# PSUM banks read from a table of their own in a table-ordered conformer block

## The chip, the cores and the metric

The kernel runs on one core of a Trainium2 chip. The metric is the device time in microseconds of one execution of the whole program. A core has five instruction streams: TensorE (PE, with weight loads shown apart as PEld), VectorE (DVE), ScalarE (ACT), GpSimd (POOL) and SyncE (SP, which here only issues DMAs). Each stream is executed strictly in the order in which the program lists it; an instruction that needs another engine's result waits on a semaphore, and everything listed behind it on its own engine waits with it.

## What is computed

A conformer block over `x` of shape (2, 4000, 144), bfloat16, with four heads of width 36:

```python
h = layernorm(x);  x = x + 0.5 * (silu(h @ w_ff1a) @ w_ff1b)          # 144 -> 576 -> 144
qkv = layernorm(x) @ w_qkv                                            # 4 heads of 36
p = softmax(q @ k.T * 36 ** -0.5);  x = x + (p @ v) @ w_o             # 4000 x 4000 per head and sequence
a, b = split(layernorm(x) @ w_pw1);  h = a * sigmoid(b)
c = depthwise convolution of h over 5 neighbours with dw
x = x + silu(c) @ w_pw2
h = layernorm(x);  x = x + 0.5 * (silu(h @ w_ff2a) @ w_ff2b)
out = layernorm(x)
```

Almost all of the work is the attention: 4 heads x 2 sequences x 4000 x 4000 scores, each of which is multiplied out, exponentiated, and multiplied with V.

## The kernel before

**Tiles.** The 8000 tokens are 16 chunks of 500 (8 per sequence), and a chunk is four blocks of 125 tokens. The keys of a sequence are 63 tiles: 62 of 64 keys and one of 32. One step of the attention takes one chunk of queries and one tile of keys for all four heads. Four matmuls of 64 x 64 weights and 500 columns (`PS<-QT,KT`) write the scores into a pair of neighbouring PSUM banks, two heads in each. Then one engine exponentiates the pair into a buffer `PT`: ScalarE in one ACTIVATE of 128 x 1000 (`emit_exp`), or VectorE in five cheaper operations that work one bank at a time (`dve_tile`). Then four matmuls (`PS<-PT,VA`) add the product with V to two accumulators, in banks 6 and 7, which are held through all key tiles of a chunk and then emptied (`epilogue`). There are 1008 such steps, 841 on ScalarE and 167 on VectorE.

Everything else is background work that is laid in between: layer norms (statistics on VectorE, `ST` and `RS`, the power on GpSimd), transposes through TensorE (`PS<-IDENT,XN`), the first feed-forward and the projections to Q, K and V (`ff1`, `pre2`), and behind the attention of a chunk its output projection, gated unit, convolution and second feed-forward (`post1`, `post2`). A feed-forward tile is two matmuls (`PS<-XT,WA`), a tanh on ScalarE (`TH<-PS`) and a product on VectorE (`HT<-TH,PS`); the way back to 144 columns is 20 short matmuls (`PS<-WB,HT`) and two additions on VectorE (`X<-PS,X`).

**PSUM.** A core has eight banks. Two are the accumulators. The other six, 0 to 5, serve the scores and all background tiles: a step on ScalarE takes two neighbouring ones (`take_pair`), everything else takes one (`take`). In the tail, behind the last attention step, bank 6 joins them.

**The order.** The program is not written down by hand: the kernel's Python plays the block through first. `Sched` holds the background jobs as generators, `pick` chooses at each step what goes next from modelled start times, `Rec.op` records each instruction with a modelled cost, and `Banks` hands out the bank that has been free the longest. `Rec.op` also finds what an instruction depends on. Its table `hist` keeps, for each key (a buffer, or `("ps", bank)`), the last writers and readers. An instruction that writes a bank depends on all who read the tile that was in it before.

What comes out is cut into blocks, one for each step of the planner and engine. Then `Rec.reorder` moves whole blocks on their engine by the table `ORDER`: one letter for each block, whose place in `ALPHABET` less 45 is the number of places by which it moves (P stays, Q goes one later, O one earlier). The dependencies stay those of the planner's play, so two tiles that the planner gave the same bank keep their turn. `Rec.finish` turns dependencies into semaphore waits and leaves out those that another wait already covers; `Rec.replay` (line 284) issues every instruction, which is why the profile gives all of them this one line.

Of the kernel before, what the change touches and what calls it, by code (L numbers as in the profile page):

```python
# [37 lines left out]
        "RPRPRRGRMOQRSQSQYIPY[GPZR[IR[GRZRY[SABBQVRUU?AEFTKPRRLMPPQRROUQJNOOPPSOPQMPPPPPPPPPQRRMNPPQSPMQNQOSO"
        "ORNOPPPPPQQNROOPQOPSPNRNOQOPPPPPPPPPPPPPPPPPPPPPPPPPPTOPNOQOTOPNVNOVNPMMOOPQOTOPSMPMQOPPQOPQOPPPPPPP"
        "PPPROOTOTPMMRNTPMORRMWPLUPVLOVQUHQHVQITQIMMPPPPPRORPMPQOPPPRRNNQOPRTQNLOPQQNPRPNQQNRPRPUPJOOOPQRNOQQ"  # L40
        "NQQRMQNPPUPNSVMMUPKMNQQMQOPSPNRNOQOTOSPMMQOQQNPQQNPSOOOPPPPPPPPPQQNPQOPQQNROOPPPPPPQOQOPPSOOOPPPPPPP"
        "PPPQOPROOSSNNRMTNOORNTNOORNTRMNSMPNSOPNTOPNQQQLQRNOQRNTNUNOSLNNQQRRLQMQQQMQOQOPPPUOPPPLQXNOOPPPPKPRS"
        "QMRLRNQSMORNWNPPQLPRTKPRSKRSSJRURISTISPSTHTHSPSJRSSHSQJRRSIRSKPSKSNSMNRNVPQQKRRRRIRJRRRLRRRJRRKRMRRM"
        "RM[QMPQXKOOOJXNLQQQKTTTINKRRSJRXKQQQJXOJPQLVOLPQLUMTOORRJQSPIQNQUNPPRLNSSNSMMOSSNNSPLQRMQRMQRRLQRLRR"
        "MQRRRJWRPJPUKTMULMMSOMQRRLSPLQRRLSPLRRMSPLRRRLWQKPPQKUPLPRRLSQRJQRKSPMQRMSPMQQRLSQMQVLPPQUKRLOMPPQOR"
        "SSSMKMPQQNUOOOOOWOOOOPPMUVNNNOMRNOQRNOQSPPLPPPPQQNQOPSOOQQMPPQOPPPPPPPPPPPPPPPPQOPPPPQQNPPPPQQQMQOPP"
        "PPPPROOROQNPPPPPPRPNPPPPPPPPPPPPPPPPPPPQOPPPPPPQOPQOPPPQOPPPPQOPPTOOOOPPSOOOPPQOPPQOPQOPSPNRPRPTQINO"
        "PPPPPPROQUMOOPNSOORPMRPNQOPRPNQQQMPPQQNPSOOQNPQOPQOPQOPSSNNNPQOPSSNNNQQNROOQQQMQQNPQOPQQQMRPNPRRN[MO"
        "PPMYNNNNVNLNOMVNPPPLVNUPULOKLQNQRNQRMUWMNNNNPQTLPRMQTLOPRMQSMORRMQQLPQORRNNPQQQSLOOPQOROOPROOPPQOQQN"
        "QQQMQRNOROOSOOQNQOQQQMQQNQQRMQQMQOQQQMQQQMQSNOQRMRNQQMPQRSOLQRMQQRLQQQLRPQMRPNROOQQNROOROOQOUOTQMMMQ"  # L50
        "RNRPMQQNPQQNROOPQQNPQQNROOPQOROOPPPPQQNPPQTNOPNRPRMOPQQNPPQQNQOQQNQQQQLROOQOQQQMQOQQQMQQQMQOPQQRMQNR"
        "PNQORPNQQNQQQMSQRNRKOPQQNROOPQQSSLRNLQOQQNQQNQQSMOQNRPSMRNNSOOZNOOOOPPMRXNLPNTUPLLLQNPQOQQNROORPNQOQ"
        "QQQQKQQQMPPRPQQQKQQNROQNPPPPPPPPPPPPQOQOPPPPPPPPPPQOPPPPPPPQOPPQOPQOPPPQOQOROOSOOSNOQNQOQQQMPPROOPPP"
        "PPQQNPPSOOOPQOPPPPPPQSNOOPQOPPPQQQMRPNPPXQNNOOPNOPTQNNOXOOOPNOORNQQSLPNQQNPPPPQQQMPQQNPQOPPPPPPQOPPP"
        "QQNRPUPPSJNNPQOPPPPPPPPPPPUOQNNQQQLQQNPPPPPPPPQQSPLOQOPRPNPQOTOPNOQOPPROQSMORNOPQOQOQOPQQNPPPQOQOQOP"
        "QQNPQOQQNQOQOQQNQQQMROOQQNQQQMSPNOQOSOOOQOPPQOPPPQOPPPQQQQQKRSQMMPROOPQRRMNPSSNNNPPPPRRRRSQRRRGGPPPP"
        "PPPPPPPPQQNPPPPPPPPPPPPPPPPPSOOOPPQOPPQOPPQOPPPPTPNOOQOQOPQQNPPQOPPPPPPPPPPPPPPPPPPPPPPPPPPPQQQQLQOP"
        "PPQOROOPQOPPQORPNQOPPQOQOPQQQRLQRMQQMPQOPROOQQNPQQNRPNPPPPSOOOPPQOPPQOPRPNQORPNQQNRPNQOPPQOPPSOOOPPP"
        "PPPPQOPPQOPQQNPSSNNNQQQMQQRMQQMQOQQNROOPPPQQQMPQVNOUNNNRMNPSPPQLQQNRPNSOPSSSNJVPPJUNNTMNRMNZPPPLPNRP"
        "MMPPPSPNOPSOPNSPNOQOPQOQOQOPROOQQNPQTNOOOPQRNQQRLQRMQQMQQRMQNQQSMRNNPRRRRUKQJRMRRLQMRRORLOPQOPQQNPQQ"  # L60
        "QMPPPPPPQOQQRMOPPPPRRNNPQORROMQQRMRNOQQQQLROOQQQMPPPPPPPROOPPQOPQOPPQOPQOPPQOPPQQNPQOSOOOPROOPPPQOQQ"
        "NPPPQQNPPPPPPPPPPQOPPPPPPPPPPPPPPQOPPPQOPQQNPPPQQNUOOOOOQOQOROOQOPPPRPQQLPPPQOPQOPQQNPPQOPPPQOPTOOOO"
        "SOOTNOOZNPXMNOULPLLLQQNRPRMOROOPVOOOOOOROQNPROQSMPRMQNQOPPPPPQOPPPPPQOPPPPPPPPRPNPQQNROOPPPPPPQQNQOP"
        "PPPPPPPPPQOPPSSNNSMROMQQQMPPPPPPPPPPPQOQTNPNQNPQRNQRRLSMPQRRSJRRKSPKQQRLQQMQOPQQNSSNNNPQOPQOPQOPVOWN"
        "QULQSSISQGIQQNVOSUSTKKTJJSSSSSMIRHOPQQNPROOQOQRPMPQSPPLQOSPNOROOPPPSOPNPPROOPROOPPPPPQQN"
    ),
    "act": (
        "PPPPPPPPPPPQRNOPPPPPPPPQOPPPPPPPPPROQNPPPPQOPPPPPPQOPQOPPPPRORNOPPPPPPPPPPPPPPPPPQQNPPPQOQOPPPPPPPPP"
        "PPPPPPPQOPPPPQOPPPPPPPPPPPPPPPPPPPPPPPPPPPPPPPPPPPPPPPPPPPPPPPPPPPPPQOPPPPPPPPQOPQOPPQOPQOPPPPPPPPPP"
        "PPPPPPPPPPPPPPPPPPPPPPPPPPPPPPPPPPPPPPPPPPQOPPPPQOPROOPSOOOPPPPPPPPPPPSSNNSMOOPPPPPPRSNNOPPPPPPPPPPP"  # L70
        "PPPPPPPPPPRRNNQQNPPPPPPPPPPPPPPPPPPPPPPPPPPPPPPPPPPPPPPROOPPPPPPPPPROOROOPPQOQOPPPPPPPPPPPPPPPPPPPPP"
        "PPPPPPPPPPPPPPPPPPPPPPPPPPPPPPPQOPPPROOPPPPPPPPPPPPPPPPPPPPPPQOPPPPPPPPPPPPPPPPPPPPPPQOPPPPPPPPPPPPP"
        "PPPPPPPQOPPPPPPPPPQQNPPQOPPPPPPPPPPQOPPPPPPPPPPPPPQOPPQOQOPPPPQOPPPPPPPQOPPPPPPPQOPPQOPPPPPPPPPPPROO"
        "PPQQNPPPPPQOPPPQOPPQOPPPPPPPPPPPPPPPPPPPPPPPPPPPPPPPPPPPPPPPPPPPPPROOPPPPPPPPPPPPPPPPPPPPPPPQOPPPPPP"
        "PPPPPPPPPPPPPPPPPPPPPQOPPPPPPPPQOPPQOPPPPPQQNPPPPPQOPPPQOPPPPPQOPPPPPPPPPPPPPPPPPPPPPPPPPPPPPPPPPPPP"
        "PPPPPPPPPPPQOPPPPPPPPPPQOPPPPPPPPPPPPPPPPPPPPPPPPPPPPPPPPPPRPNPPPQRNOPPPPPTOOOOPQOPPPPPPPPPPPPPPPPPP"
        "PQOPQOPPPPPPPPPPQOPPPPPPPPPPPPPPPPPPPPPPPPPPPPPPPPPPPPPPPPPPPROOPQOPPPPPQOPPQOPPPPPPPQOPPPQOPPPPPPPP"
        "PPPPPPPPPPPPPPPPPPPPPPQOPPPPPPPPPPPPPROOROOPQOPPPPPPPPPPPPPPPPPPQQNPPQQQMPPQOPPQOQQQQQQJPQO"
    ),
    "dve": (  # L80
        "PPQOPPQOPPPROOcOOOR`MMMNQMMMPMMZOMTPPHUQRLTRPWRBOTEOMNPSOOOQOPQQQSQKQMWRPNLOOOPPPPPTOOOQNPPPVPPQQTQQ"
        "TTFPGRRRNQRGQNPUPRUNKMXNYMOQOKOQJNPPR[NNOYNZMMMMMMQQKRKRNOPQOPPPQOQQNPQOQSNOOPQOPPPPPPPPPPPPPPPQRRRR"
        "KRKQNRPNPTPPPTPTOOSOPQRPQQQQQQQQSPSS5RSQRTJSSESSKRJ^PPJOOOOOOOQNNQOPQOPPPPPROQNQOPPPPPPQOQOQOPPTRSMR"
        "LQKPPPPPQQNQOPPPPPPPPPPPPPQOPPPPPPPPPPQOQOQOPQOSQNNRVNNPN`NNOOOPNZNNNNNNNNOOQOPPPPQQQMPQOROSNRNQMPPP"
        "PPPPPPQQNPPPPPPPPPSPNOROOQOPPPPPPPSOOOPTPPSLPSPKSNORNORPNSPNSNOSNROMPPPPPRPNROOQOROQQMQOPQOQORPNROOR"
        "OQQQLPPPQOPPQOPQOPSOPNQOPQQNPQOPPPPPRPSMPNROORPNPRPNQOQQN[OPNQNNPNOPNPPPROOPPPQOPPPPPPPPPPPPPPPPPPPP"
        "PPPPPPPQOPPPPPPPPPPQOPPPQOPPPPPPPPPPPPQQNPPPPPPQOQRPSPKOPPPPPQOPQOPPPPPPPQOPPPQOQOQOPPPPPPPPPQQNPPQO"
        "PPUOOOTOTLNNRNOSOPSPLRNQNPPPPQRNOPPPPPPPPPPPPPPPPPPPPPRRRMQQKPSOTOMOQNPPPPPPPPPPROQNPQOPPPQOPPPPPPPP"
        "PPYOOOOOOOOORTRMMNPPPPPPPPPPQOQOPPPPPPPPPQOQOPQQRMQQQQQQSHPQMPPQOPQQQMPQQNROUNOOOOPQOPPPPPPPPQOUOPNO"
        "OPTOQRMMPPPPPPPPPPPPPPPPPPPPPPPPPPPPVPQMPPLPQQQMPPPPPPQOPPQOPPPPPPQOPPPPQOPPPPPPPQOQOPQOPSPNRNOQQNQR"  # L90
        "NOPSOPNoOOOOOOOOOOOOOOOOOOOOOPNOOOPNPNQOPPPPPPPPQOPROOROOSPROQKPPPPPPPPPPRPRMQQQQKPPQOPQQNPPPPPPPPPP"
        "PPPQOPPPPPPPPPPPPPQQNPPQOPPP_OOOOROQLPLPNPNPWORNNNPNPPPPPPQOPPPPPPPPSORORLOPPQORPNPQOPQQQMQOPPPPPPPQ"
        "QQMPPPQOPQOQRNQNPQOPPPPPPPQOQOPPQQQRPKPPQQNPQQNPRPQMPPPPPPPPPPQOPPPPPROQNPRPNROOQOPQOQQNPQOPQORPQQLR"
        "RNQMPPSPNOPPTPNPQQLQQNPPPPPPPPPPPPPPQOQOPPPPQOPPPQOPPPPQOQOPPPPPPQOUOPNRNQMPPROOPPPPPPPPPPPPPPPPPPPQ"
        "QRPQQQIPPROOPROQNQOPPPQQNPPQOPPPPPPPPPPPPROQNPRPQMQOPPPPPPPPPPPPPPPPPPQOPQOPPPPQQQMPRORPRPKPPPPPPPPR"
        "OQQQLPPRPNPPPPPPPPPPPPPQOPPPPP^ROSLPLPLOOOOOROOQTTPLMNPQOPQRTOPROISOOOWPQORPNQHQOPTOSOTLMOORPNQOPQOP"
        "PPPPPPPPPQQQM"
    ),
# [12 lines left out]


# [1708 lines left out]
```

## Time and profile before

| | |
|---|---|
| median of three runs | 910.52 us (910.25 to 910.66) |
| the profiled execution | 910.27 us, span 908.5 us |
| granted TensorE clock | 0.998 of full speed |
| instructions in the profile | 27,451 |
| TensorE matmuls and weight loads | 11,946 each |
| ScalarE / VectorE / GpSimd busy | 871.8 / 807.8 / 276.1 us |
| exponential on ScalarE, 128 x 1000 | 825 times, mean 1060 ns from start to end |
| exponential on VectorE, 128 x 500 | 334 halves, mean 671 ns for the first operation |

How to read it: instructions of one engine overlap at their ends, so the mean duration of an instruction is longer than the distance at which they follow each other, and busy time counts overlapped time once. Matmul ends are modelled. A wait in the table of waits is idle time of the waiting engine, put down to the instruction that came last. The chain is followed back from the last instruction of the program, at each step to what released it.

### The profile page before, as it was taken

What the parts mean: (1) busy time and instruction counts of PE and PEld (TensorE: products, weight loads), DVE (VectorE), ACT (ScalarE), POOL (GpSimd) and SP (SyncE); (2) the same over time, 40 slices, a digit from 0 to 9 for tenths busy, and PEclk for the clock granted to TensorE, in tenths of its full rate; (3) what the DMA queues carried; (4) which work ended last, traced back from release to release, by engine and by line L of the source; (5) the groups of instructions that cost most, each with busy time, mean ns of one, the idle gap of its engine ahead of it and who ended that gap; (6) DMA issues with size and microseconds to landing.
All of it is one profiled execution on the core that took longest, in us unless ns stands there. A gap on an engine that the chain in (4) does not pass through costs nothing.

```text
span 908.5 us, 27451 instructions
## 1 busy us (share of the span) xinstructions
PE 883.6 (97%) x11946; PEld 410.0 (45%) x11946; DVE 807.8 (89%) x1756; ACT 871.8 (96%) x1105; POOL 276.1 (30%) x519
## 2 busy tenths in 40 slices
...
## 3 DMA queue, kind: packets, MB, share of 16 engines
...
q10 hardware_dynamic: 1416, 0.62, 0.3%
...
## 4 chain that ended last, share of the span: by engine, by line
ACT 50%; PE 43%; DVE 5%; issue 1%; DMA 0%; POOL 0%; POOLq 0%; DVEq 0%
ACT PT L284 45%; PE PS L284 43%; ACT TH L284 5%; DVE PT L284 2%; DVE ST L284 1%; DVE HT L284 0%; DMA X<-in_x_dram 0%; POOL RS L284 0%; DVE X L284 0%; DVE KT L284 0%; DVE QT L284 0%; DVE VA L284 0%; DVE U L284 0%; DVE XT L284 0%; DVE XN L284 0%
## 5 line engine op out<-in xcount | busy, mean ns | idle before, releaser
L284 ACT ACTIVATE PT<-PS 128x1000 bf16<-128x1000 f32 (+1 forms) x841 | 776.9, 1052 | 6.6 <-PE PS L284 3.7
L284 PE MATMUL PS<-QT,KT 64*64 64x500 bf16 x3968 | 418.7, 385 | 11.8 <-ACT PT L284 7.4
L284 PE MATMUL PS<-PT,VA 64*37 64x500 bf16 x4636 | 401.7, 373 | 1.6 <-DVE QT L284 0.8
L284 DVE TENSOR_SCALAR PT<-PS 128x500 int16<-128x500 f32 x334 | 222.4, 671 | 25.0 <-PE PS L284 22.6
L284 PEld LDWEIGHTS PS<-QT,KT 64*64 64x64 bf16 x3968 | 122.7, 104 | 220.3 <-ACT PT L284 119.8
L284 PEld LDWEIGHTS PS<-PT,VA 64*37 64x37 bf16 x4636 | 134.1, 96 | 93.3 <-DVE PT L284 20.7
L284 POOL TENSOR_SCALAR RS<-ST 125x4 f32<-125x4 f32 x112 | 34.1, 304 | 465.3 <-DVE ST L284 459.5
L284 DVE TENSOR_SCALAR PT<-PT 128x1000 uint16<-128x1000 uint16 x334 | 136.1, 417 | 2.6
L284 POOL TENSOR_SCALAR XN<-X,RS 125x144 bf16<-125x144 bf16 x224 | 130.9, 596 | 6.5 <-DMA out_dram<-XN 0.8
L284 POOL TENSOR_TENSOR RS<-RS,NHALF 125x4 f32<-125x4 f32 (+1 forms) x101 | 95.5, 950 | 92.7 <-DVE RS L284 87.9
L284 DVE TENSOR_TENSOR PT<-PT 128x1000 bf16<-128x1000 bf16 x167 | 112.8, 678 | 1.9
L284 ACT ACTIVATE TH<-PS 128x500 bf16<-128x500 f32 (+3 forms) x198 | 104.4, 547 | 6.0 <-PE PS L284 4.5
L284 DVE SCALAR_TENSOR_TENSOR HT<-TH,PS 128x500 bf16<-128x500 bf16 (+1 forms) x135 | 81.5, 618 | 19.2 <-ACT TH L284 18.5
L284 PE MATMUL PS<-XT,WA 72*128 72x500 bf16 (+2 forms) x280 | 71.9, 359 | 0.4 <-DVE VA L284 0.2
L284 DVE SCALAR_TENSOR_TENSOR X<-PS,X 125x288 bf16<-125x288 f32 x128 | 57.5, 452 | 13.3 <-PE PS L284 11.9
L284 DVE BATCH_NORM_STATS2 ST<-X 125x6 f32<-125x288 bf16 (+1 forms) x160 | 66.3, 448 | 0.9 <-DMA X<-in_x_dram 0.6
L284 PE MATMUL PS<-WB,HT 128*125 128x144 bf16 (+1 forms) x640 | 52.3, 230 | 0.1
L284 PEld LDWEIGHTS PS<-WB,HT 128*125 128x125 bf16 (+1 forms) x640 | 44.2, 136 | 14.0 <-issue 5.4
L284 DVE COPY XT<-PS 72x1000 bf16<-72x1000 bf16 (+2 forms) x65 | 40.1, 618 | 5.6 <-PE PS L284 4.9
L284 PE MATMUL PS<-IDENT,XN 125*72 125x125 bf16 x512 | 42.9, 221 | 1.3 <-DVE XN L284 1.0
L284 PEld LDWEIGHTS PS<-IDENT,XN 125*72 125x72 bf16 x512 | 32.0, 112 | 20.5 <-issue 10.9
L284 PEld LDWEIGHTS PS<-XT,WA 72*128 72x128 bf16 x280 | 19.7, 97 | 31.5 <-DVE HT L284 7.7
...
## 6 DMA issues: line engine op xcount, KB each, us to landing
...
```

Of the source, the lines that this page charges most:

```text
L284: ins = getattr(eng, o.name)(*o.a, **o.k)
```

## The change

The bank of a tile is no longer the one that the planner hands out. The planner still plays with its own numbers, now called slots; `Banks.take` and `take_pair` give out `Place` objects, integers that carry the real bank, the slot and the number of the tile. The real bank is read from a new table: `PLACES` holds one figure for each of the 1778 tiles, in the order in which the planner takes them, and a pair takes that bank and the next. `Rec.plain` maps a key back to its slot, so that `hist`, and with it every modelled time and every choice of the planner, is the same as before.

While it records, `Rec.sort` notes for each dependency whether it is there only since two different tiles share a slot (`shared`) or for a reason of its own (`own`). `Rec.reorder` drops the first kind. Then it goes through TensorE's list in its new order, finds for every tile which tiles were last in its banks, and lets its TensorE instructions depend on all instructions of other engines that touch those tiles. So a bank's turn follows the final order of TensorE, not the planner's.

All five strings of `ORDER` are replaced as well: the string for TensorE has 2885 letters in place of 2888, ScalarE 1095 in place of 1091, the others keep their length. Of TensorE's letters some 1,750 differ from those before; 1,794 blocks move (before: 2,065).

```diff
 ORDER = {
     "pe": (
-        "PPPPPPQOPPPPPPPQOPPPQQQQLPPPPQOPRPNRPNQQNPPPWOfNNNcMQMPMINPNLNNOMOMNNPTPNOOPPPPRPNPPROORRUMMPNRTMNRO"
+        "PPPPPPPPPPPPQQRROKPPPPQQNQOQOPQOPPPPQOPRPNQOeOxRMMzPRKLHMNROMKMEOQLJOOQOIQKNQKMOOKOMOMNOOQNQQLQTNOYN"
...
 }
+PLACES = (
+    "0354231433401042510103542035202535024054032151540442105303210412543053121304124010241122402043124032"
...
+    "2140205240240120420421412041204120412041204021402420154250420524025405240524025405240524052405230423"
...
+    "052405245052402402102243002642340643521630254350615436214506230156245130546130"
+)
 
+class Place(int):
+    pass
 
 class Rec:
     def op(self, eng, name, *a, r=(), w=(), q=None, cost=0.1, kind=None, lat=None, **k):
...
+        o.tile, o.shared, o.own = None, set(), set()
+        for key in tuple(r) + tuple(w):
+            if isinstance(key[1], Place):
+                o.tile = key[1].no
         for key in r:
-            h = self.hist.setdefault(key, ([], []))
+            h = self.history(key)
             o.deps += [(d, True) for d in h[0]]
+            self.sort(o, key, h[0])
             h[1].append(o)
...
+    def place(self, slot, n):
+        no, at = len(self.tiles), int(PLACES[len(self.tiles)])
+        self.tiles.append(tuple(range(at, at + n)))
+        out = []
+        for j in range(n):
+            p = Place(at + j)
+            p.slot, p.no = slot + j, no
+            out.append(p)
+        return tuple(out)
+
+    def plain(self, key):
+        return (key[0], key[1].slot) if isinstance(key[1], Place) else key
+
+    def sort(self, o, key, ds):
+        for d in ds:
+            if d is not o:
+                other = isinstance(key[1], Place) and d.tile is not None and d.tile != o.tile
+                (o.shared if other else o.own).add(id(d))
 
     def reorder(self, table):
...
             lines[e] = [o for blk in at for o in blk]
+        users = {}
+        for o in self.ops:
+            drop = o.shared - o.own
+            o.deps = [(d, raw) for d, raw in o.deps if id(d) not in drop]
+            if o.tile is not None and o.eng != "pe":
+                users.setdefault(o.tile, []).append(o)
+        last, prior = {}, {}
+        for o in lines["pe"]:
+            k = o.tile
+            if k is None:
+                continue
+            if k not in prior:
+                prior[k] = {last[b] for b in self.tiles[k] if b in last}
+                last.update({b: k for b in self.tiles[k]})
+            for p in prior[k]:
+                o.deps += [(d, False) for d in users[p]]
...
 class Banks(Slots):
     def take(self):
         i = self.choose()
         del self.free[i]
-        return i
+        return self.R.place(i, 1)[0]
 
     def take_pair(self):
         i = self.pair()[2]
         del self.free[i], self.free[i + 1]
-        return i, i + 1
+        return self.R.place(i, 2)
```

More of the change, by code (lines that the diff above doesn't have):

```diff
@@ L36 @@
     "pe": (
-        "PPPPPPQOPPPPPPPQOPPPQQQQLPPPPQOPRPNRPNQQNPPPWOfNNNcMQMPMINPNLNNOMOMNNPTPNOOPPPPRPNPPROORRUMMPNRTMNRO"
[L38 to L65, printed above, removed]
+        "PPPPPPPPPPPPQQRROKPPPPQQNQOQOPQOPPPPQOPRPNQOeOxRMMzPRKLHMNROMKMEOQLJOOQOIQKNQKMOOKOMOMNOOQNQQLQTNOYN"
@@ new lines @@
+        "NOSQTQKKTPQRSQWQ^BRW`EPWQ[GQ[EQ]RY]S?BBRWSZU?CCFUGQVTHKKNQSPPXPHQQNLOSNPQMPPPPPPQOPRRRMMPPPTPNPNQOSO"
+        "PQMPPQOPPPPPPQOPQOQSNPRPLQOPPPPPPPPPPPPPPPPPPPPPPPPPPQOPPPPPQOPPQOPQOPPPPPPPPQOPPQOPPPQQNPPQOPPPRPRP"
+        "RROIQOSQSQLLQOSOPNQQNSOOUPTLPVQUJQIWQKSQIMMTPPPLTPPROQSQHRMOQOPROOPPQOROOQQNPROOQQNQOPPTOOOOPPPPPPQQ"
+        "NPPPPQQNPPQOPQQNPQOPPPQOPQOPQOQOPPPPPPPPPPPPPQOPQOPPPPPPPPPPPPPPPPPPPQSNPQRLOPPPPPPPPQOPQQNPPPPPQOPP"
+        "PQQNPPPQTNOOQNPPPPPPPPPPPPPQRPMQOPPQOPPTOOPNQQNPROOSSNNNUPNSNOMQQQRLUNOOOOROOPROOPPPPQOPSPNQNQQQMPPS"
@@ new lines @@
+        "OOQNPPPRPNQOUPNOPNPPROOQQNQQQMPRPNQRNQNPQORPQMQOPQQNQOPPPQOPPPPPPPPPQOPQOPQQNPPPPPPPPPPQOPPPTOOOOSOP"
+        "RPSKOOQTNOORNTPMORRMRRRKRLRRRLRRKRRRKSQKRRLTPLTOMRNQMQQSMSNROLQQSMOOQQNQQNQSNPRRLNROOQQNPQOQQQMSPNQQ"
+        "MQQQRLQQQLQSNROULPNRNNQQQMROOQQQMRPNQQNQQNQQQMQRNQQRLQRMQQRLRPSLPRMSPMQRMSPMQRRLQRLQQMQRRTLPLTNOPRMQ"
+        "QQTKPNQQTLPNQQRLQNQQRRRKTTKNNQMRPNPPPPQOQQNQOPROQNQOPQOQOQOPQQNPPPPPPPPPPPPPPPPPPPPPPPPPPROOPPPPQOPP"
+        "PPPPROOPSOPNPPPPPPROOPPPPPPPPPPPPPPPPPPQOPPPPPPQOPQOPPQQNPPPPPPPPPQOPPPPPPPPPPPPPPPPQOPPSPNRPRPQQIPP"
@@ new lines @@
+        "WOOOOQRMQRKOQOQWNOQNNRNNROQNQOPQQNPPPQOPPPPQOPPPROOPPPPPPPPPPPQOPPPPPPPPPPPPPQOPPPPPQOPPPQQNPPPPPPPP"
+        "PPPROOPPRPNPPPPPPPPPPPPPTOQNNPPPQOPQOTUPMMNOQQSMOQNQTNOORNQSMOQSMSOMQQMRROMQSSSSKMKQQNPRPNROOPPPPQQN"
+        "PQQNPQOPSPNOPPSOOOPPPPROOPPQOPPPPPPPPPPPPPPPPPPPPRSQSLLOPPQOPQOPQQNPPQOQOQOQOPPQOQOPQOPQOPPPPPPPPPPP"
+        "QOPQOPPPPPPPQOPPPQOPPPPPQOPPPQOQOSQNQQLPPPPPPPPRORNOPPPPPPPQOPPPQOQQQQLROOQOQQQMQOQQQMQQQMQOQQQQLPPP"
+        "PPPPPPPPPPPPPPQOPPQOQOPRPNPPPPPQRNVNOQNNQNRPNQQSMOQNRPQMRPNSOOQNQOPPPSOOTNOOOPQOQQQQLPQOQQNROOQQNQOQ"
@@ new lines @@
+        "QQQQKQQQMPPRPQQQKQQNROQNPPPPPPPPPPPQQNQOPPPQQNSPNOPPSPRRLMPQOPPQOPQOPPPQOQOROOSOOSNOQNQOQQQMPPROOPPP"
+        "PPQQNPPSOOOPPPPPPPPPPSOOOPPPROOQQRMQNPQOPPPPQQNPPPPPPPPPPPPQOPPQOPPSOOOPQOTQNNOPQOPPQOQQNPPPPPUPNYNY"
+        "MMNVNUOPSHIIPQOPPPQQNPQOPPUOQNNQQQLPPPPPPPPPPPQQSPLOQOPRPNPQOTOPNOQOPPROQRMOPQOSOPQMROOQQNPPPRPNPQOP"
+        "PPPPPPPPPPPPPPPPPPPPPPPQQNPPQOPPPPQOPPPPPPPPPPPPPPPPTPPPQQQITUSMMMMQOQOQQNRRSSLLNQOPROOPPPPQOROOPPQQ"
+        "QQQKPPQQQQLPPPPPPPPPPPPPPPPPPPPPPPPPPPPPPPPPPQQNSQNTRLNQMPPQOPPQOQOPPPPSSPSQKKQOQQQMQQQMQQQMQRNOQOPQ"
@@ new lines @@
+        "RNOSPNQQQLQQQMQOQQNPQQNPPPQQQQLRVNNOOOOPRSNNQQMQQQMTOOOOPPPPSQNNQOPPQOPRPNPPTRNNNPRPNQOPPQOPPSOOOPPP"
+        "PPPPPQOPQOPQQNPSSNNNPQQNPQRNQQMQOQQNROOPPQQQQLPQSNOQNQRNOSORNNQOPQOQOPQOPPQRPMQTTMNNNSOOQNPPQOQOPPPQ"
+        "OPROOPQOPPPPPPPPPPPPPPPPPPPPSOPNQOPPRPNQOPPQOPQQNQQNRPNPQQNQOQQQMROOQOPRRSMRLRMQQMQOSPPRLOPQOPQQNPPP"
+        "QOPPPPPPPPPPPPPPPPPRRNNPPPPRPNRPRMRNOPPQQNROOPQQNPPPPPPPPRPNQQNROOPQSNOQNPRRNSPLQNPQOPPQOPPQOPPPQOQQ"
+        "NPPPQQNPPPPPPPPPPQOPPPPPPPPPPPPPPQOPQOQOQOQOPPPPPPPPQOPPPPPPQOQOQOPPQOROOQQQQLQQNQRRMQMROOPQQNQRPMQO"
@@ L66 @@
+        "ZQOXLNNWMPXKKOUIOLNNQSNPNQQNROOPVOOOOOOQOROQQMQRPMQOPPQOPPPPPQOPPPPPPQOPPPPQOPQOSOPQMROOPPPPQOPPPPPP"
+        "PPPPPPPPUOQNNRSMNSNROMPPQOPPPPPPPPPPPQOPQOQOQOPPQOQRRMRMOQRRRLTPKRNNQQQMPSOOOPQQNPSOOOPPPQOPPRPNVPUM"
+        "QSLRRRIRRGNPQOZOPX_WKLPKKKKQQQSPGUIOOPNPQOROOPPPQOPSQOMPPPPPPPPPPPPROOPPPROOPQOPPPPQO"
     ),
     "act": (
-        "PPPPPPPPPPPQRNOPPPPPPPPQOPPPPPPPPPROQNPPPPQOPPPPPPQOPQOPPPPRORNOPPPPPPPPPPPPPPPPPQQNPPPQOQOPPPPPPPPP"
-        "PPPPPPPQOPPPPQOPPPPPPPPPPPPPPPPPPPPPPPPPPPPPPPPPPPPPPPPPPPPPPPPPPPPPQOPPPPPPPPQOPQOPPQOPQOPPPPPPPPPP"
@@ L70 @@
[L70 to L78, printed above, removed]
+        "PPPPPPPPPPPPROOPQQNPPPPPPPPPPPPPQRSMNOPPPQOQQNQOQQSMPSMOOPPQOQOPPPPPPPPPPPPPPPPPPQRNOPROOPPPPPPPPPQO"
@@ new lines @@
+        "PPPPPPPPPPPPPPPPPPPPPPPPPPPPPPPPPPPPPPPPPPPPPPPPPPPPPPPPQOQQNQQNPPPPQOPPPPPPPPPPPPPPPPPPQOPPPPPPPPPP"
+        "PPPPPPPPPPPPPPPPPPPPPPPPPPPPPPPPPPPPPPPPPPQOPPPPPPPQOPPQOPPPPPPPPPPPPPQQNPQOPPPPPPPPPPPPPPPPPPPPPPPP"
+        "PPPPPPPPPPQQNPPPPPPPPPPPPPPPPPPPPPPPPPPPPPPPPPPPPPPPPPPQOPPROOPPPPPROOQOPPPPPPPPPPPPPPPPPPPPPPPPPPPP"
+        "PPPPPPPPPPPPPPPPPPPPPPPPPPPPPPPPPPPPQOPPPPPPPPPPPPPPPPPPPPPPPPPPPPPPPPPPPPPPPPPPPPPPPROOPPQRNOPPPPPP"
+        "PPPPPPPPPPPPPPPPPPPPPPPPPPPPPPPPPPPPPPPPPPPPPPPPPPQOPPPPQOPPPPQOPPPPPPPPPPPPPPPQOPPPPPPPPPPPPPPPPPPP"
@@ new lines @@
+        "PPPQOPPPPPQOPPPQOPPQOPPPPPPPPPPPPPPPPPPPPPPPPPPPPPPPPPPPPPPPPQOPPPPPPPPPPPPPPPQOPPPROOROOPPPQOPPPPPP"
+        "PPPPPPPPPPPPPPPPPPPPPPPPPPPPPPPPPPPPPPPPPPQQNPPPPPPPPPPQOPPPPPPPPPPPPPPPPPPPPPPPPPPPPQOPPPQOPPPPPPPP"
+        "QOPPPPPPPPPPPPPPPPPPPPPROOPPPPPPPPPPPPPPPPPPPPPPPPPPPPPPPPPPPPPPPPQOPPPPPPQOPPPPPPPPPPPPPPPPPPPPPPPP"
+        "PQOPQOPPPPPPPPPPQOPPPPPPPPPPPPPPPPPPPPPPPPPPPPPPPPPPPPPPPPPPPPPPPPPPPQOPQOPPQOPPQOPPPQOPPPQOPPPPPPPP"
+        "PPPPPPPPPPPPPPPPPPPPPPQOPPPPPPPPPPPPPQOPQOPPPPPPPPPPPPPPPPSSNNNQQNROOPPPPPQQNPPPQRPQQQQIPQOPPQO"
@@ L79 @@
     ),
     "dve": (
[L81 to L95, printed above, removed]
@@ L96 @@
-        "OQQQLPPRPNPPPPPPPPPPPPPQOPPPPP^ROSLPLPLOOOOOROOQTTPLMNPQOPQRTOPROISOOOWPQORPNQHQOPTOSOTLMOORPNQOPQOP"
-        "PPPPPPPPPQQQM"
+        "PPROQQQLPQOPSOOOPPQZNOOORNNNPNPVOPRORKSQOJ`PPMQOQQNPIQOMOOPQOSPTTTOJNJQWROLNOOOQQQRRKNPVOQQNSOSOTQTP"
+        "QTBSHOSPROSHUNQ[LQYMJNNNWPMKQQJQUQJPT[KMNXO_KMMNNRPRHQIQLSMPNPPPQOQQNPQOPPPPPPQOPPPPPPPQOPPPPQQQQRTQ"
+        "NROQQRROQQQQQQQQQQQQQQQQQRRRTTPPSQSS$RRCQQZRRGQQKRJWNPKOPPMiOOOOOOPNPNOOOOOQNPMOOOOOPPPPPPPQOPPROQNP"
+        "PPPPPPPRSOMOPPPPPPPPPPPPPPPPPPPPPPPQOPPPPPQQQQQTQOPQFQOQOWOPNPNPNZWNPMMOMNNOPPPPPPPPQOPSORNSMRNQMPPP"
@@ new lines @@
+        "PPPPPPQQNQOPPPPPPPPPPPPPPQOPPPPPPPSORNQRSQRISQOIPPPQOPPQOPQOQOPRPSPLOPPPPQOPQRNRNQNQQNQOPQOPPPPPQQNQ"
+        "OPQOPPQOQOPPPPPPPPPPPPPQOQQNPQOPPPPPPQQNPPRPNPPPQSNOOPPPPTOPNQNQOQOQOPPPQQNPPPPPPPQOPPPPPPPPPPPPPPPP"
+        "PPPPPPQOPPPPQOPPPPPQOPPQQNPPPPPPPPPPPPQOPPPPPPPQOQQQQQKPPPPPPPPPROOPPPPPPPPROOPQOPQOPPQOPPPPPPQOPPPP"
+        "PPPQOQOPQOPPPPPPPPPQOROQNPPPPQQNPPPPPQOPPQOQOPPPPQOPPRRSQLQQJPRPUROQNIPPPPPPPQOPYOOOOPNOOSNOOPPPPPPP"
+        "PP[PNOOOOPPPPSQOHPPPPPPPPPPPQOQOPQOQOPPPPPPPPPPPROQQQQQQTHPPMPPQOPQOPPPPQOPPPPQQNPPPPPPROOPQOQOUOOOO"
@@ new lines @@
+        "OPPPPPPPPPPPPPPQOPPPPPPPPPPPPPPPPPQOPPRORPMROQQMPPPPPPQOPPQOROOPPPROOPPPQOQOPPPQOPPQOPPQOQOQQNPPPPPP"
+        "PQOPPPPVOQNPMOQOPPPPQOQOQRROLQOPPPPPROOPPPPPPPPPQOPQOPRROTPQOQHQOPPPPPPPPPPPRPNPQOPQQNPPPQQNPPPPPPQO"
+        "QOPPPPPPPPPPPPPPPPPPPPPQOQOPPPPPPPPPPPPPPPPPTOQNNQOPQOPPPQOPPROOPPPPPPRORNOQOPPQOPPPPPROQNPRPNQOPPPP"
+        "QQQMROQNPROQRMQNPROQQMPPPPPROOPPQQQSPKOPRPNPQORORNQNPPPPPPPPPPPPPPPPPQOQOPPQOQOPPPROOPQOPQOQRNQQQQKQ"
+        "QNQOPPQQNPQOSQOQQQJRPNPQOPPPPPPPPPPROOQOPPPPQOQOPQOPPPPQOPQOQOQOPPPUOOOSNPMQOROOQOPPPPPPPPPPPPPPPPPQ"
@@ L98 @@
+        "QNPPROOPPPPPPPPPPQOPPPQQNPPPPPPPPPPSOOOPPROQNQQVPLPNORNOPPPPPPPPPPPPPPPPPPPPPPQOPQOQOQRNQNPPPPPPPPPR"
+        "OQRPLPPRPNPPPPPPQQNPPPPQOPQOPQZSORKQLPKOOPPSQRSLPRPUHOOOOPPPPPQOPPSOOOVOOOOOOPPQOPSPSOSKNOPRPRRRKQLQ"
+        "QQQLPQOPPQQQM"
     ),
     "pool": (
-        "PQQQRPQQRPQSQOQQQQQQRPQQQRPQQQQQQQQQRPQQQRP%QOYOOOOOOSNORPQQIPPSQNQMPQZUQQKLSTJSKTKUUNNOFQUPQJNOPPTR"
-        "NVMMOWPNPKORNQMPRPQMPPPPPQO"
+        "PQQQQQQQRPRROQQQQQQQRPQQQQQQQQQQQQQQRPQQQQS%OOROOPPPPQQNSPPQLPTWNNNRMVZRTJJLSKLNNVOUNNOOLPTOWNNUMNPN"
@@ L102 @@
+        "LRPQMUUNNPMRPQJQRPQLPPPPPQO"
     ),
     "sp": (
-        "PPPPPPPQOPRPN"
+        "PPPQQNPPPPROO"
     ),
 }
+PLACES = (
+    "0354231433401042510103542035202535024054032151540442105303210412543053121304124010241122402043124032"
+    "4202422034302430224034203420354052042405240524501240120421402141204124042504250425042504240214021401"
+    "2140205240240120420421412041204120412041204021402420154250420524025405240524025405240524052405230423"
+    "0240342034204320340243023024120412041214021412041250425042504254052405240253052305350425052405240524"
+    "0542301440520452405204520524504250425052405425042504250425042540524052405240542042504250425042504250"
+    "4220305240540120402412041204120412041021402140214021402140214021402140120412041204102140214021420412"
+    "0412041210421403245013501315351305130510351035023205320534023401430243024302430243024203430243024302"
+    "4302342034203404201224304034034203420342043024302430243042302430243024302342034203420340234203240324"
+    "0324032402340324045030255240520452405204250425042504250425405240524052405240524052405240524052405240"
+    "5240524052405235043023450424024502405250425042504204250425042304304303430224302340324024024230423042"
+    "3024302430242034203420342301530205305350232053205320524504250250520452404250425404250425042405240525"
+    "0425042502405240524025042150120420420420140214024120425042540524052504240124024020412041021402140214"
+    "0214021402140214021404212054052405240250425042405240524052540524053103502405420420425042505235023502"
+    "3502530530535023502350232053012532033024042033402340342034204302430243023430420342024304302430420342"
+    "0324302430243024024014014320143203420430423024304203423024302430243013401430143143134021043104320342"
+    "0342034203420342034203420245025024025042504250425042504520425042504250424052405235053205304250524042"
+    "5025025052405244020421042142045204250452042042405240524055241240124012041205402540524052504250240542"
+    "052405245052402402102243002642340643521630254350615436214506230156245130546130"
+)
@@ L121 @@
 class Op:
-    __slots__ = ("eng", "name", "a", "k", "idx", "deps", "clock", "inc", "waits", "cnt", "q", "done", "t0", "t1", "kind", "step")
+    __slots__ = ("eng", "name", "a", "k", "idx", "deps", "clock", "inc", "waits", "cnt", "q", "done", "t0", "t1", "kind", "step", "tile", "shared", "own")
+class Place(int):
+    pass
 class Rec:
@@ L144, in __init__ @@
         self.step = 0
+        self.tiles = []
         self.filling = False
```

11 lines of the change are left out of this document (7 added, 4 removed).

## The prediction

> **What bounds the kernel now.** I began with the first and fourth part of the page, the busy shares and the shares of the chain that ended last.
>
> ```profile
> PE 883.6 (97%) x11946; PEld 410.0 (45%) x11946; DVE 807.8 (89%) x1756; ACT 871.8 (96%) x1105; POOL 276.1 (30%) x519
> ACT 50%; PE 43%; DVE 5%; issue 1%; DMA 0%; POOL 0%; POOLq 0%; DVEq 0%
> ```
>
> No engine bounds the kernel alone. Half of the chain lies on ScalarE, 43% on TensorE, and VectorE is 89% full. DMA and GpSimd carry nothing of it. Next I cut the span into front, first half of the body, second half and tail with the table of windows (columns: window, length, then busy time and instructions of PE, PEld, DVE, ACT, POOL, then clock, DMA share, GB/s).
>
> ```profile
> 0.00:75.00 75.00, 71.42 (x925) 42.96 (x925) 66.42 (x202) 61.96 (x98) 23.58 (x48) 1.00 0.16 46
> 75.00:325.00 250.00, 246.24 (x3346) 105.42 (x3349) 224.34 (x463) 244.26 (x295) 70.67 (x133) 1.00 0.01 2
> 325.00:850.00 525.00, 515.43 (x7022) 227.90 (x7014) 468.43 (x954) 522.33 (x644) 163.31 (x305) 1.00 0.02 5
> 850.00:908.50 58.50, 50.53 (x663) 33.73 (x662) 48.62 (x139) 43.20 (x71) 18.55 (x33) 0.97 0.05 14
> ```
>
> ScalarE is idle for 13.0 us in the front, 5.7 and 2.7 us in the two parts of the body, and 15.3 us in the tail. But its busy time hides stalls, which two other views show: the groups with shapes kept apart, and the chain in order of time (start, length, what).
>
> ```profile
> L284 ACT ACTIVATE PT<-PS 128x1000 bf16<-128x1000 f32 x825 | 769.3, 1060 | 5.7 <-PE PS L284 2.9
> 227.46 14.92 PE PS L284 x196
> 764.63 27.42 ACT PT L284 x31
> ```
>
> Where ScalarE is never kept waiting, 31 exponentials take 27.42 us, 0.884 us each. Over the whole span one costs 769.3 / 825 = 0.932 us of busy time, since a late start does not overlap with the end of the one before. So I took the starts of neighbouring ScalarE instructions from the timeline and subtracted the shortest step that ever follows that shape (0.884 us for 128x1000, 0.467 for 128x500, 0.259 for 128x250, 0.155 for 125 columns). What is left is time that ScalarE lost: 14.7 us in the front, 15.8 us in 75 to 325, 18.2 us in 325 to 850, 17.1 us in the tail. The loss in the body, 34.0 us, is what a better order could take away at most. It is denser in the first part (0.063 us per us) than in the second (0.035), and there the chain lies on TensorE for long pieces, as the 14.92 us at 227.46.
>
> The waits say what TensorE waits for (us in total, times, longest), and one stretch of the timeline shows how such a wait reaches ScalarE.
>
> ```profile
> PEld PS L284 <- ACT PT L284: 126.5, 352, 1.2
> PEld PS L284 <- DVE PT L284: 66.4, 220, 0.7
> PEld PS L284 <- DVE HT L284: 22.7, 65, 0.8
> ```
>
> ```profile
> 192.20 1.90 ACT L284 ACTIVATE PT<-PS 128x1000 bf16<-128x1000 f32 x2 [0.20 <-PE PS L284]
> ...
> 192.51 1.31 PEld L284 LDWEIGHTS PS<-WB,HT 128*125 128x125 bf16 x20 [0.35 <-DVE VA L284]
> ...
> 193.90 0.11 PEld L284 LDWEIGHTS PS<-QT,KT 64*64 64x64 bf16 x2
> ...
> 194.83 2.10 ACT L284 ACTIVATE PT<-PS 128x1000 bf16<-128x1000 f32 x2 [0.73 <-PE PS L284]
> ```
>
> At 192.5 the 20 residual matmuls stand 0.35 us until VectorE has emptied a V tile out of a bank. They then run for 1.3 us, the next scores start behind them, and ScalarE stands idle for 0.73 us. A bank wait of TensorE becomes a ScalarE stall because TensorE takes its list strictly in order. This is the wait that the change can touch.
>
> **The change, part by part.** (1) What stays. The planner still keeps its bank numbers by slot, and its costs, its choice of the 167 tiles that VectorE exponentiates and the 841 that ScalarE does are computed as before. So every engine issues the same instructions with the same shapes, and only their order, the banks and the semaphore waits differ. Busy work is costed at no change: a repeated form varies little (the shortest ScalarE step behind a 128x1000 tile is also the median one, 0.884 us).
>
> (2) Banks alone. I laid the kernel's list of tiles, with the bank of each, over the starts in the trace. In the body 4.98 of the six banks are held on average. TensorE had nothing running and started a tile within 0.13 us of the release of its bank 177 times, 27.8 us in all: 20.5 us before 111 score pairs and 7.3 us before 66 single tiles. In 41 of the 177 another suitable bank stood free earlier, and taking that one would have saved 4.3 us. In the other 136 every suitable bank was still held. TensorE carries 43% of the chain, and a wait while ScalarE is the late one costs nothing, so 4.3 x 0.43 = 1.8 us.
>
> The Trainium skill (Perfetto Trace Analysis, Optimization Strategy) says that the same bubble repeating on an engine that should be full can mean too little PSUM for the next tile. The 4.98 held banks agree with it. By that rule alone renumbering six banks makes no room and the sum stops at these 1.8 us; it is the second rival below.
>
> (3) The order that the banks set free. Before, two blocks whose tiles share a planner bank can't pass each other on TensorE. Afterwards the list is free in this, and the bank's turn follows the list. The new TensorE letters differ from the old in 60% of their places (about 1,750 of 2,885), so nearly the whole order is new. Its bounds are 0 (waits only change places) and 7.1 us, which is what falls away if 75 to 325 comes down to the density of the second part: 15.8 - 250 x 0.0347 = 7.1. I take the middle, 3.5 us: the cause shown at 192.5 is an order of this kind, but VectorE at 90% and TensorE at 98% of that window allow no order without stalls.
>
> (4) Added waits. An instruction of TensorE with two conditions gets a separate semaphore instruction; the trace has 55 of them on TensorE at 51 ns. A pair whose two banks were last read by different engines needs such a second condition. Twice as many cost 55 x 0.051 = 2.8 us, none at all gains the same, and both only where TensorE is on the chain. I take 0, since the new table mostly repeats cycles of four figures (0524, 2403), in which the same banks come back as pairs. Behind a waiting instruction the whole TensorE list is queued, then ScalarE and VectorE, which wait for its scores.
>
> (5) Front and tail. The front's letters move blocks by up to 41 places, and eight late tiles now use bank 6. The first exponential starts at 19.6 us behind a chain of loads, norms and the first feed-forward; the tail is TensorE alone for 37.7 us on the chain. Their losses of 14.7 and 17.1 us are mostly such chains, and three or four late steps of the size seen (0.35 to 0.73 us) are worth 2 us either way at each end. I take 0.
>
> (6) GpSimd and SP get new letters too. GpSimd is 30% busy and SP stores only finished rows, so they cost nothing as long as VectorE's next statistics don't wait for them; without that cover, one GpSimd row of four (304 to 1,124 ns) would be late by its own length.
>
> Sum: 1.8 + 3.5 = 5.3 us against the profiled execution of 910.27 us (908.5 span and 1.8 around it; the median of the runs is 910.52, 0.25 more). That gives 905.0 us. No difference under 0.2%, 1.8 us, can be told from no change here.
>
> **The rivals.** Larger gain: the cause at 192.5 is everywhere, and half of the body's 34.0 us falls away, 910.3 - 17 = 893 us. For it speaks that the stalls are many and small (149 over 0.05 us, 27.5 us together), against it that TensorE was running in nearly all the time before them: only 6 of the 149 had TensorE idle for over a third of the 1.9 us before. The Trainium skill (Perfetto Trace Analysis, Identifying the Most-Contended Engine) takes the busy share of ScalarE as a fair measure of its distance to the limit. By that rule the body has only the idle 8.4 us to give and no time under 901.9 us is open; the row with 0.932 against 0.884 us disagrees with it.
>
> Only the banks: order gains and losses cancel, 910.3 - 1.8 = 908.5 us, which is no difference. For it speaks that banks are full in 136 of 177 waits.
>
> Slower: the new turn puts scores behind a bank whose reader is late. A feed-forward tile that VectorE empties holds its bank 2.28 us at the median and 5.19 at most, a convolution tile 3.5 and 6.8, a score bank 1.7. VectorE empties over 800 single tiles, and a score pair placed next behind one of the long ones stops the whole TensorE list. The price is the wait seen at 192.5, 0.35 us. It decides from 15 such waits on (5.3 / 0.35); with 30 on the chain it is 910.3 - 5.3 + 10.5 = 915.5 us. Against it speaks that the shapes' durations are so even that a bank's turn can be laid out ahead; for it, that in the waits VectorE already ends 66.4 and 22.7 us of TensorE's idle time, in 285 pieces, so it often is the late reader.
>
> **How the numbers follow.** Forecast 905 us (about 899 to 908.4): 0.48. Larger gain (under 899): 0.14. Only banks or nothing (908.4 to 912.1): 0.10. Slower: 0.28, half of it beyond 915. So faster 0.62, same 0.10, slower 0.28. The range runs from 897 to 915 us: it leaves out half of the slower case, 0.14, and less than half of the larger gain, 0.06. The forecast's own range is 899 to 908.4 us.
>
> **What would show it.** Right: the loss of ScalarE between starts falls from 15.8 us in 75 to 325 to some 11 us, the exponential's busy time per instruction falls below 0.932 us, the wait of PEld for DVE readers (66.4 and 22.7 us) shrinks, and counts and shapes stay. Term (2) is right if the tiles that wait while another bank is free become fewer than 41. The prediction is wrong if TensorE's waits for DVE PT or DVE HT grow with ScalarE's idle time behind PE PS, if the semaphore instructions on TensorE rise well over 55, or if the difference lies in the front or tail windows and not in the body.

## The result

The changed kernel takes 905.54 us (905.49 to 905.59, median of four runs) against 910.45 us before. The ratio is 0.9946 with a 95% interval of 0.9929 to 0.9963, so 4.9 us are gained. The forecast was 905.0 us. The profiled execution took 905.58 us, its span 903.7 us.

The engines of the page after (first part, and the chain's shares):

```profile
PE 878.2 (97%) x11946; PEld 409.1 (45%) x11946; DVE 808.1 (89%) x1756; ACT 869.2 (96%) x1105; POOL 278.5 (31%) x519
ACT 48%; PE 42%; DVE 6%; POOL 2%; issue 1%; DMA 0%; POOLq 0%; DVEq 0%
```

Every engine runs as many instructions as before (TensorE's separate semaphore instructions, which these counts leave out, rise from 55 to 80). TensorE's busy time falls by 5.4 us. The windows of the profile after, cut at the same times (same columns as in the prediction):

```profile
0.00:75.00 75.00, 71.57 (x934) 43.63 (x935) 66.34 (x203) 62.88 (x99) 23.74 (x48) 1.00 0.16 46
75.00:325.00 250.00, 247.64 (x3400) 107.61 (x3401) 226.57 (x471) 246.64 (x299) 73.70 (x133) 1.00 0.01 2
325.00:850.00 525.00, 512.69 (x7029) 226.27 (x7025) 470.81 (x955) 521.60 (x647) 163.11 (x306) 1.00 0.02 5
850.00:903.70 53.70, 46.30 (x603) 31.60 (x591) 44.38 (x129) 38.12 (x63) 17.97 (x32) 0.95 0.05 15
```

In the same 250 us from 75 to 325, TensorE now does 3,400 matmuls where it did 3,346, and ScalarE is busy for 246.64 us, 2.4 us longer. From 325 to 850 both do what they did.

Since both kernels issue the same instructions, I compared the start of each ScalarE instruction in one trace with the start of the same one in the other (means over 12 us). The changed kernel is 1.1 us ahead at 75 us, 1.7 at 175, 3.0 at 275, 4.5 at 325, 4.4 at 500 and 4.8 at the end. Nearly all of the gain is made before 325 us.

For the same work up to that place (4,266 matmuls start before 325 us in the trace of before), TensorE had no matmul streaming for 61.5 us where it was 65.6 (each matmul counted from its start at 0.42 ns a column, which the pairs of score matmuls show: 2 x 416.1 us busy / 3,968 / 500 columns), and 3.3 us of these 4.1 come from gaps longer than 0.2 us. It changes between kinds of matmul 349 times instead of 352, so fewer changes explain little.

The stretch shown in the prediction stands at 189 us now (timeline of the profile after):

```profile
189.42 0.11 PEld L353 LDWEIGHTS PS<-QT,KT 64*64 64x64 bf16 x4 [0.31 <-ACT PT L353]
189.76 1.31 PEld L353 LDWEIGHTS PS<-WB,HT 128*125 128x125 bf16 x20 [0.22 <-DVE VA L353]
...
191.15 0.14 PEld L353 LDWEIGHTS PS<-QT,KT 64*64 64x64 bf16 x6
...
191.61 1.00 ACT L353 ACTIVATE PT<-PS 128x1000 bf16<-128x1000 f32 x1 [0.26 <-PE PS L353]
```

The residual's matmuls wait 0.22 us for the V tile's bank, not 0.35, and ScalarE stands still for 0.26 us, not 0.73.

The totals of the waits move far less (waits of the profile after):

```profile
PEld PS L353 <- ACT PT L353: 127.4, 371, 1.1
PEld PS L353 <- DVE PT L353: 69.0, 209, 0.7
PEld PS L353 <- DVE HT L353: 18.6, 51, 0.6
```

Beside 126.5, 66.4 and 22.7 us before, no one would see the gain in them. My reading is that the difference lies in which of the waits were on the chain; no run shows that by itself.

### The profile page after: what moved, and what is told of

It is laid out like the page before. It is cut to its first block, busy times and chain, and to the rows that moved or that the text cites. A ratio compares the mean times of both kernels' runs of the same rounds, so it can differ in the third digit from the quotient of the medians.

```text
span 903.7 us, 27474 instructions
## 1 busy us (share of the span) xinstructions
PE 878.2 (97%) x11946; PEld 409.1 (45%) x11946; DVE 808.1 (89%) x1756; ACT 869.2 (96%) x1105; POOL 278.5 (31%) x519
## 4 chain that ended last, share of the span: by engine, by line
ACT 48%; PE 42%; DVE 6%; POOL 2%; issue 1%; DMA 0%; POOLq 0%; DVEq 0%
ACT PT L353 43%; PE PS L353 42%; ACT TH L353 5%; DVE PT L353 3%; POOL RS L353 1%; POOL XN L353 1%; DVE ST L353 1%; DVE HT L353 1%; DMA X<-in_x_dram 0%; DVE QT L353 0%; DVE XN L353 0%; DVE XT L353 0%; DVE KT L353 0%; DVE X L353 0%; DVE RS L353 0%
## 5 line engine op out<-in xcount | busy, mean ns | idle before, releaser
L353 PE MATMUL PS<-QT,KT 64*64 64x500 bf16 x3968 | 416.1, 385 | 10.7 <-ACT PT L353 6.0
L353 PE MATMUL PS<-PT,VA 64*37 64x500 bf16 x4636 | 394.6, 373 | 2.1 <-DVE PT L353 0.9
L353 PEld LDWEIGHTS PS<-PT,VA 64*37 64x37 bf16 x4636 | 131.9, 96 | 95.9 <-DVE PT L353 22.0
L353 ACT ACTIVATE TH<-PS 128x500 bf16<-128x500 f32 (+3 forms) x198 | 107.0, 563 | 3.3 <-PE PS L353 2.1
L353 DVE SCALAR_TENSOR_TENSOR HT<-TH,PS 128x500 bf16<-128x500 bf16 (+1 forms) x135 | 81.1, 616 | 18.8 <-ACT TH L353 18.4
L353 DVE SCALAR_TENSOR_TENSOR X<-PS,X 125x288 bf16<-125x288 f32 x128 | 57.2, 451 | 12.4 <-PE PS L353 10.9
L353 PEld LDWEIGHTS PS<-IDENT,XN 125*72 125x72 bf16 x512 | 31.8, 112 | 23.4 <-issue 11.4
```

Of the source, the lines that this page charges most:

```text
L353: ins = getattr(eng, o.name)(*o.a, **o.k)
```

## Experiments

All were measured in turn with the kernel before, whose medians were 910.5 to 910.7 us; each gain is counted from the median beside it. In the short diffs, "new" and "old" are the strings of the change and of before.

**e1 and e2: which stretch gains.** The lists are cut at the place that the profile of before reaches at 325 us (TensorE's block 976, ScalarE's 389, VectorE's 586).

```diff
-ORDER, PLACES = new, new
+ORDER  = {e: new[e][:cut[e]] + old[e][cut[e]:]}      # e2: old first, then new
+PLACES = new up to the cut, the planner's bank behind it
```

> The new order and banks for everything up to the place where the profile of before stands at 325 us, the old order and the planner's banks behind it. Theory (the gain is made in the first part, where ScalarE lost most): 905.5 to 906.5 us, nearly all of the change's 4.9 us. Rival (the gain is spread over the body, a lead won early is lost again at the first place where an engine is full): 908 us or more.

> The other half: the old order and the planner's banks up to 325 us, the new order and banks behind it. Theory: 910.0 to 910.7 us, no difference from before, since in the change the lead over before stays at 4.4 to 5.1 us from 325 us on. Rival (the new tables also gain behind 325 us and only lose it to something carried over from the first part): 908.5 us or less.

Measured: e1 905.83 us, ratio 0.9949 (0.9937 to 0.9962); e2 911.03 us, ratio 1.0006 (0.9997 to 1.0014). e1 came out as its theory said. e2 lies 0.3 us above its theory's range, on the side of no gain, and cannot be told from before. The lead of e1 over before is 4.5 us at 325 us and 4.3 us at the end: a lead made early is kept. The new tables behind 325 us are worth nothing that can be measured.

**e5: the new rule for waits alone.**

```diff
-        no, at = len(self.tiles), int(PLACES[len(self.tiles)])
+        no, at = len(self.tiles), slot
 ORDER = old
```

> The order of before and the planner's own banks (each tile takes its slot as its bank), with only the new way of finding waits: a bank's turn is read from TensorE's final order. 74 of 11,946 TensorE instructions then carry another set of conditions than before. Theory: 910.0 to 910.9 us, no difference, so that what e1 to e4 show belongs to banks and order. Rival (the old dependencies held back TensorE where two tiles of one slot had changed places): 909 us or less.

Measured: 911.04 us, ratio 1.0005 (0.9996 to 1.0013). By the median that is 0.5 us slower than before, just outside the theory's range, but the interval holds no difference. So the rule gains nothing by itself; it only makes other orders and banks possible.

**e3 and e6: banks alone, under the old order.**

```diff
 ORDER = old
-PLACES = ("0354231433401042510103542035202535...
+PLACES = ("0120321400121243510021354024505232...      # e3
+PLACES = ("0120321401230354021341203413040313...      # e6: few double conditions
```

> The order of before on all engines, instruction for instruction, but every tile's bank chosen anew, so that on the starts and ends of before's trace TensorE would wait least for banks (39.3 us of bank waits in place of 48.0 with the planner's banks, each counted alone). Theory (the prediction's term 2, banks alone): a gain of 1 to 3 us, 907.5 to 909.5 us. Rival A (banks alone make the whole gain): 905 to 906 us. Rival B (the waits only move to the next full bank): 910.0 to 911 us.

> As e3_old_order_new_banks, with the banks chosen so that TensorE's instructions rarely wait on two engines at once: 59 instead of 125 instructions with two conditions, bank waits of 40.0 us instead of 39.3 by the same count. Theory (the prediction's term 4 is real where TensorE is on the chain: 66 x 0.051 x 0.43 = 1.4 us): 907.2 to 908.2 us. Rival (a second condition is hidden, since the instruction is waiting anyway): 908.8 to 909.4 us, as e3.

Measured: e3 909.06 us, ratio 0.9984 (0.9975 to 0.9993), a gain of 1.4 us; e6 908.85 us, ratio 0.9981 (0.9972 to 0.9990). Banks alone gain a little. TensorE's separate semaphore instructions fall from 127 in e3 to 61 in e6 and the difference of 0.2 us is inside both intervals: a second condition costs nothing that can be measured here, and e6's theory falls.

**e4, e7 and e8: other banks under the new order.**

```diff
 ORDER = new
-PLACES = ("0354231433401042510103542035202535...
+PLACES = ("0123450123402401523452301432005304...      # e4: the bank empty for longest
+PLACES = ("0120312400131453210103540143202535...      # e7: fewest bank waits
+PLACES = ("0120312402041405312325342035202303...      # e8: the same, few double conditions
```

> The new order on all engines, but every tile takes the bank that has been empty for longest by the trace of the change, with no thought for pairs that come later. On that trace's starts and ends 43 tiles then come late, by 14.1 us in all. Theory (a bank's turn decides where TensorE's list stops, the prediction's third rival): 5 to 14 us slower than the change, 910 to 919 us. Rival (the order makes the gain, the banks hardly matter as long as six of them turn): 905.5 to 907 us.

> The new order on all engines, with banks chosen on the trace of the change as those of e3 were on that of before: bank waits of 37.6 us instead of 42.9 by the count on that trace, but 123 TensorE instructions with two conditions instead of 78. Theory (banks act in the new order as in the old one, where 8.7 us fewer counted waits gained 1.4 us): 904.3 to 905.3 us. Rival (the table of the change fits its order so well that any other costs time): 906 us or more.

> As e7, but with 59 instructions with two conditions and counted bank waits of 38.3 us. Theory (both terms act): 903.0 to 904.5 us, faster than the change and than e7. Rival (second conditions are hidden): the same as e7 within 0.5 us.

Measured: e4 915.16 us, ratio 1.0051 (1.0039 to 1.0064); e7 905.51 us, 0.9943 (0.9930 to 0.9955); e8 905.47 us, 0.9942 (0.9930 to 0.9955). In e4 the waits of the ScalarE exponentials for scores grow, and so do TensorE's matmul waits for those exponentials (first fence e4, second the profile after):

```profile
PE PS L353 <- ACT PT L353: 12.2, 34, 1.0
ACT PT L353 <- PE PS L353: 9.3, 23, 1.1
```

```profile
PE PS L353 <- ACT PT L353: 6.0, 16, 0.8
ACT PT L353 <- PE PS L353: 4.0, 9, 1.2
```

So taking the bank that has been empty for longest, with no thought for coming pairs, costs 9.6 us and turn the gain into a loss. (The planner's own rule is another one: of the banks that came free within 0.3 us of the first, `choose` takes the one that leaves most pairs.) But banks with 5.3 us fewer counted waits than the table of the change gain nothing more: e7 misses its theory's range by 0.2 us, and it is not slower than the change either, as its rival would have it. Its 123 instructions with two conditions are not to blame, since e8 with 59 takes the same time; e8's theory of a faster kernel falls. The banks of the change do as well under this order as the two tables chosen by the count, and they are not the only ones that do.

**e9 and e10: the new order with the planner's banks.** The table differs from the planner's numbers for just 200 of 1,778 tiles, and just 8 pairs of tiles that follow each other in a planner's bank change their turn in the new order. That suggested that the order alone might do it.

```diff
 ORDER = new
+# e9: PLACES = the planner's slot, except for 18 tiles
+# e10: program of before; the old order stays in the first 50 us, the tail, six short stretches
```

> The new order on all engines. The table of the change gives 200 of the 1,778 tiles another bank than the planner did; here 182 of these go back to the planner's bank, and only the 18 stay without which TensorE's list and the waits would form a ring. Theory (the order makes its gain only with banks that turn with it): counted on the trace of the change, bank waits rise from 42.9 to 94.2 us; in e4 12.8 us more by this count (55.7) cost 9.6 us, so 30 to 45 us slower than the change, 935 to 950 us. Rival (the gain is the new order's own, and the table is only needed where the order would otherwise stand still): 905 to 907 us.

> The program of before with no table of banks, and of the new order all that its planner's banks allow: 1,561 of TensorE's 2,889 blocks stand elsewhere than before. The old order stays for about the first 50 us, the tail and six short stretches between them. Theory: the same bank waits as in e9 where the order is new, without the front's share, so over 915 us. Rival (the new order is merely a better one, which the old scheme could have had): 906 to 908 us, the gain behind the first 75 us, 3 to 4 us.

Measured: e9 958.4 us (950.56 to 964.81), ratio 1.0522 (1.0452 to 1.0593); e10 935.68 us, ratio 1.0271 (1.0255 to 1.0286). The rival falls: this order without its banks, or nearly this order in e10, is 25 to 48 us slower than before. Even the theory's 935 to 950 us for e9 was too little. The waits and the clock show why (two waits of e9 and one of e10; the clock line of e9's page, 40 slices; two windows of 4 us of e9, same columns as above):

```profile
PEld PS L353 <- DVE HT L353: 27.8, 53, 2.3
ACT PT L353 <- PE PS L353: 24.8, 42, 1.6
```

```profile
ACT PT L285 <- PE PS L285: 21.0, 33, 2.7
```

```profile
PEclk9889999999999999999999999799999999999999
```

```profile
40.00:44.00 4.00, 2.54 (x16) 1.36 (x15) 1.93 (x6) 1.17 (x2) 0.00 (x0) 0.70 0.00 0
44.00:48.00 4.00, 4.00 (x27) 2.76 (x26) 1.34 (x3) 2.23 (x4) 0.00 (x0) 0.50 0.00 0
```

In e9 the exponentials wait 24.8 us for scores where it was 4.0, and TensorE's granted clock falls to half, which it never does in the body before or after. The trace of e9 has seven such stretches ahead of the tail, 37.5 us in all. At half speed they cost up to 18.8 us of TensorE's work (37.5 / 2, an estimate), which the count of bank waits did not hold. The four runs of e9 agree: they go from 950.56 us at a mean granted clock of 0.988 to 964.81 us at 0.965, and a straight line through them gives some 945 us at the 0.998 of before, an estimate that lies in the theory's range. In e10 the clock falls for 10.2 us at 583 us and for 6.8 us in the tail, at most 8.5 us of its 25 by the same working (17.1 / 2), so most of its loss is waits.

## Why the prediction was right, and where it was not

**Place and size.** Right. The first part of the body was named as the place, since ScalarE lost most there per microsecond and the chain lay on TensorE; that part gave 3.4 us and the front 1.1.

**The count of ScalarE's loss** was taken wrongly in the prediction: for the 128x250 shape the sums used a step of 0.084 us (one odd pair) and not the 0.259 us that the text names. With 0.259 the loss before is 11.2, 14.6, 15.9 and 11.4 us for the four windows, 30.5 us in the body. After, it is 10.2, 10.9, 15.6 and 11.7. The 0.155 us for 125 columns is not right for both shapes either: it is the shortest step behind 80x125, and behind 64x125 the shortest is 0.298 us, which takes another 2.1 us off the body (28.4 us before, 24.3 after). The upper bound of term 3 hardly changes (14.6 - 250 x 0.0303 = 7.0 us), and the drop in 75 to 325 is 3.7 us by either count.

**Term 2, banks alone, 1.8 us.** e3 gives 1.4 us (0.6 to 2.3 by its interval), and some 2 us beside e5, which finds its waits by the same new rule. The size held, its working did not quite: choosing all banks anew takes away 8.7 us of counted waits, not 4.3, and a sixth of that reaches the end, not 43%. The other way round it is dear: in e4, 12.8 us more by the same count cost 9.6 us. My reading, which no run shows by itself: a wait taken away is mostly followed by the next limit, ScalarE or VectorE, while a wait put in stops all three.

**Term 3, the order, 3.5 us.** The rest of the 4.9 us is 3.5 us. e3 and e7, whose banks were chosen by the same count, each for its own order, differ by 3.6 us (909.06 and 905.51), so the term holds as the prediction built it, banks first and then the order with banks to suit. That its size was met so closely is luck: 3.5 was the middle between bounds of 0 and 7.1. And the gain isn't the order's own. What the sum of two terms hides is that they can't be had apart: e10 shows that nearly this order with the planner's banks costs 25 us, and e3 that good banks with the old order gain 1.4 us. Only the pair gains 4.9 us. The reading that "nearly the whole order is new" also misled: most letters move, but of the turns in a planner's bank only 8 change. What the table frees is not these turns, it is the bank of 200 tiles that would come late.

**Term 4, waits.** TensorE's semaphore instructions rose from 55 to 80, 1.3 us at 51 ns if all counted. e6 and e8 show that they don't, so this sign of a wrong prediction was none. Nor do they come from the table: e5, with the old order and the planner's banks, has 78, so nearly all come from the new rule for waits.

**Term 5, front and tail.** Taken as 0 with 2 us either way; the front gained 1.1 us and the tail nothing. The eight late tiles in bank 6 are nothing new, since the planner gave them that bank too.

**Term 6, GpSimd.** The cover was taken as enough, and in one place it isn't. GpSimd now has 2% of the chain (before 0%), and behind 379 us the chain goes over it (chain of the profile after):

```profile
379.55 2.32 POOL RS L353
382.28 3.16 POOL XN L353 x4
385.49 27.08 PE PS L353 x424
```

There TensorE waits 1.45 us for GpSimd's normalised rows. The lead over before falls from 4.7 us at 365 us to 3.0 at 395 and is at 4.1 again from 410 on, while in e1, which has the old order there, it stays at 4.5. So the new order loses about half a microsecond here, which later stretches win back.

**The rival of the banks only.** The Trainium skill (Perfetto Trace Analysis, Optimization Strategy) says that the same bubble repeating can mean too little PSUM for the next tile. A forecast by that alone would have ended at a gain of 1.8 us. Banks held in the body are 5.01 on average (before 4.98), so no room was made, and the kernel still gained 4.9 us: in these runs it mattered which bank a tile takes, not how many are held.

**The slower rival** was right that a bank given back late stops TensorE's list, and e4 takes 915.16 us, where the rival was priced at 915.5 us. That the two agree is chance. The price was 30 waits of 0.35 us for readers on VectorE, but in e4 TensorE's matmul waits for ScalarE's exponentials grow (6.0 to 12.2 us), and its weight loads wait 18.8 us for VectorE's DVE HT against 18.6. VectorE as the late reader shows in e9, where that wait is 27.8 us. The change stays clear of both because its banks suit its order.

**The signs to look for.** Tiles that wait while another bank is free fell from 41 to 33. ScalarE's loss in 75 to 325 fell by 3.7 us, where 4.8 was forecast (15.8 to 11). But the exponential's busy time per instruction didn't fall (769.5 / 825 = 0.933 us, before 0.932), and TensorE's waits for VectorE's two readers fell only from 89.1 to 87.6 us, the part for DVE PT even rising from 66.4 to 69.0. Those signs were too coarse.

What stays open: which of the 200 tiles carry the gain; which engine's new letters do, since no run takes over the order of one engine alone; and how much more an order and banks chosen together could give. e7 and e8 only show that two tables with fewer counted waits add nothing to this order.
